# The second unit's decays from stacked rows, the first rows loaded between two halves of a weight block, two fills moved to GpSimd, other dummy matmuls

## The chip, the cores and the metric

The kernel runs on one core of one Trainium2 chip. The metric is the device time of one execution in microseconds (us). A profile of one execution comes with it: it says for each engine (TensorE, called PE, with its weight loads PEld; VectorE, DVE; ScalarE, ACT; GpSimd, POOL; and the DMA queue of SyncE, SP) what ran when and what it had waited for.

## What is computed

A chunked state-space scan over 4 batches, 8 heads and 768 positions, followed by a two-layer network. With `la = log(clip(a))`, and in every chunk:

```python
cum = np.cumsum(la, axis=-1)
L = np.exp(cum[:, :, :, None] - cum[:, :, None, :]) * causal
M = np.einsum('bhin,bhjn->bhij', Cc, Bc) * L
y = np.einsum('bhij,bhjd->bhid', M, xc) + (C state) * np.exp(cum)
state = exp(sum la) * state + sum_j (B_j x_j) * np.exp(cum[-1] - cum[j])
...
h = x @ w_in                      # 3072 x 256 times 256 x 2048
g = np.maximum(0.01 * h, h)
out = g @ w_out                   # 3072 x 2048 times 2048 x 256
```

The kernel takes chunks of 96 positions (`Q`), not of 32, which gives the same values.

## The kernel before

**Units.** The scan is cut into 32 units, each one chunk of 96 positions of one batch with its 8 heads. Unit `u` is batch `u % 4` of chunk `u // 4`. For each unit there are four steps:

1. *Decays.* PE writes the exponents of `L` (112 rows by 8 heads by 96 columns) into a PSUM tile `pd`; ACT takes the exponential into `lt` (`decay_of`, L276).
2. *Scores.* `scores` (L321) multiplies C and B for 4 heads at a time into a PSUM tile `sc`, of which there are two; DVE multiplies each half by `lt` (L326, two instructions).
3. *Products.* `unit_products` (L348 and L357, 8 small matmuls each) gives y and the new state in a `pd` tile, of which there are also two.
4. *Out.* ACT copies the state (`stage`, L381) and y (`xh`, L386), DVE takes the low part (`xl`, L391), and POOL carries the state into the next chunk's operand (L384).

**Three ways to the decays.** Units 0 and 1 (`DIRECT = 2`) go a direct way: a mask matmul in bf16 (`decay_mask`, L239), then an fp32 matmul with `reach`, a masked copy of `la` that POOL makes (`fill_reach`, L199; `decay_direct`, L246). Units 2 to 15 go by stacked rows (`decay_pe`, L265): one bf16 matmul for each half, whose operands `dl` and `dr` hold 0/1 masks and, in some of their rows, the cumulative sums of `la`, each split into three bf16 pieces. These rows are made so: PE sums (`sum_rows`, L221), DVE splits (`split_sums`, L227 to L230), one DMA stores the pieces to DRAM (`parts_d`, L618), and `decay_load` loads them back twice for a number of units, into `dl` (L254) and into `dr` (L257). There are 8 slots (`SLOTS`) for units; four units' rows at a time are loaded again later. Units from 16 on take their decays from a broadcast load. This change does not touch them.

**The order.** The order of instructions on each engine is written out by hand: no scheduler moves them. Each engine runs its own list in order and waits by semaphores; a DMA is issued in its place in the list of SP or ACT, and an issue that has to wait holds up what stands behind it on that queue. The prologue (L602 to L637) does the sums, the first units' decays and the first loads. The loop after it (L638) takes units 0 to 9: for unit `u` it does the decays of unit `u + 2`, the scores of unit `u + 1`, and the products of unit `u`, and in between parts of the decoding of the network's weights, which arrive as 64-bit floats in blocks of 512 KB (`fetch_w`, L100, into `raw`). After that the network's matmuls (`ffn_in`, L554, and `ffn_out`, L578) start, and the other units are woven between them.

**Dummies.** `keep_warm` (L128) issues matmuls of zeros, whose result is not used.

Of the kernel before, what the change touches and what calls it, by code (L numbers as in the profile page):

```python
# [13 lines left out]
U32 = mybir.dt.uint32  # L14
# [3 lines left out]
NB, NH, S, D, N = 4, 8, 768, 32, 16  # L18
Q = 96
# [9 lines left out]
B_COLS = NB * QE  # L29
LAG = 3  # L30
WARM = 6
WARM2 = 2
RAWS = 3
SHIFT = 448
LOAD = 4
# [9 lines left out]
POOLED = (0, 1, 2)  # L45
DRAWN = 3

DIRECT = 2
SLOTS = 8

STACKED_AT = {12: 0, 14: 2}
# [17 lines left out]
def scan_ffn(ctx: ExitStack, tc: tile.TileContext, a_l, b_l, c_l, bn_l, x_l, w_l, out_l):  # L69
# [25 lines left out]

    raws, bcs, xss, bns = {}, {}, {}, {}

    def fetch_w(f, eng=nc.sync):
        raws[f] = wr.tile([128, 2 * DM, 2], U32, name="raw")
        eng.dma_start(raws[f].rearrange("p c w -> p (c w)"), w_l[f].bitcast(U32))  # L100

    ccs = [pst.tile([128, 2, NB, Q], F32, name=f"cc{i}") for i in range(2)]

# [15 lines left out]
    def fetch_x(c, eng=nc.sync):  # L119
        eng.dma_start(xss[c][:Q].rearrange("p b c -> p (b c)"), x_l[c])  # L120
# [5 lines left out]
    def keep_warm(space, n):  # L126
        for _ in range(n):
            nc.tensor.matmul(  # L128
                space.rearrange("p (a b) -> p a b", b=128), lhsT=idle,
                rhs=idle.unsqueeze(1).to_broadcast([128, 4, 128]), start=True, stop=True,  # L130
            )
# [10 lines left out]
    for c in range(3):  # L142
# [35 lines left out]
        out=less, in_=less, pattern=[[3, NH]], compare_op=ALU.is_ge, fill=0.0, base=Q + 2,  # L178
        channel_multiplier=-1,
    )  # L180

    def fill_first():
        nc.vector.tensor_copy(dr[:Q, 0], later.unsqueeze(1).to_broadcast([Q, NH, Q]))

    def fill_less():
        rows = slice(Q, Q + 3 * NH)
        nc.scalar.copy(dr[rows, 0], less[rows].unsqueeze(2).to_broadcast([3 * NH, NH, Q]))

    def fill_slots(lo, hi):
        rows = slice(0, Q + 3 * NH)  # L190
        nc.vector.tensor_copy(
            dr[rows, lo:hi].rearrange("p b h i -> p b (h i)"),
            dr[rows, 0].rearrange("p h i -> p (h i)").unsqueeze(1).to_broadcast(
                [Q + 3 * NH, hi - lo, NH * Q]
            ),
        )

    def fill_reach(u):
        nc.gpsimd.affine_select(  # L199
            out=reach[u], in_=la[:, u * NH:(u + 1) * NH].unsqueeze(2).to_broadcast([Q, NH, Q]),  # L200
            pattern=[[0, NH], [1, Q]], compare_op=ALU.is_ge, fill=0.0, base=0,
            channel_multiplier=-1,
        )
# [33 lines left out]
    def decay_mask(space):  # L237
        for g in range(2):
            nc.tensor.matmul(  # L239
                heads_of(space, g), lhsT=upto_b,  # L240
                rhs=later.unsqueeze(1).to_broadcast([Q, NH // 2, Q]), start=True, stop=False,
            )

    def decay_direct(u, space):
        for g in range(2):
            nc.tensor.matmul(  # L246
                heads_of(space, g), lhsT=after, rhs=reach[u][:, 4 * g:4 * g + 4],
                start=False, stop=True,
            )

    def decay_load(u, n, eng=nc.sync):
        p, b = u * NH, (u - DIRECT) % SLOTS
        rows = parts_d[p:p + n * NH]
        nc.sync.dma_start(  # L254
            dl[Q:Q + 3 * NH, b:b + n, :Q], rows.rearrange("(u h) t i -> (h t) u i", h=NH)
        )
        eng.dma_start(  # L257
            dr[Q + 3 * NH:KD, b:b + n].rearrange("t b h i -> t (b h) i"),
            rows.rearrange("r t i -> t r i"),
        )  # L260

    def decay_pe(u, space):
        b = (u - DIRECT) % SLOTS
        for g in range(2):
            nc.tensor.matmul(  # L265
                heads_of(space, g), lhsT=dl[:KD, b], rhs=dr[:KD, b, 4 * g:4 * g + 4],
                start=True, stop=True,
            )
        decay_of(u, space)
        after_u = u + SLOTS - LOAD + 1  # L270
        if (u - DIRECT + 1) % LOAD == 0 and after_u < STACKED:
            decay_load(after_u, min(LOAD, STACKED - after_u))

    def decay_of(u, space):
        lt = lts[u] = plt.tile([QE, NH, Q], F32, name="lt")
        nc.scalar.activation(  # L276
            lt.rearrange("p (g h) i -> p g (h i)", g=2), space[:QE, :, :4 * Q], AF.Exp
        )
# [23 lines left out]
    def state_decay(c):  # L302
        nc.gpsimd.tensor_tensor(
            out=bns[c][:, :NB * NH * N].rearrange("p (h n) -> p h n", n=N),
            in0=bns[c][:, :NB * NH * N].rearrange("p (h n) -> p h n", n=N),
            in1=erev[:, c * NB * NH:(c + 1) * NB * NH].unsqueeze(2).to_broadcast([QE, NB * NH, N]),
            op=ALU.mult,
        )
# [3 lines left out]
    def scores(u, warm=0):  # L312
        c, b = divmod(u, NB)
        lt = lts[u].rearrange("p (g h) i -> p g (h i)", h=2)
        for half in range(2):
            sc = score_tile()
            if half == 0 and warm:
                keep_warm(sc[:, 0], warm)
            for g in range(2):
                r = 32 * (2 * half + g)  # L320
                nc.tensor.matmul(  # L321
                    sc[:QE, g, :2 * Q].rearrange("p (k i) -> p k i", k=2), lhsT=bcs[c][r:r + 32, b * QE:(b + 1) * QE],
                    rhs=ccs[c % 2][r:r + 32, :, b], start=True, stop=True,
                )
            heads = lt[:, 2 * half:2 * half + 2]
            nc.vector.tensor_tensor(out=heads, in0=sc[:QE, :, :2 * Q], in1=heads, op=ALU.mult)  # L326
# [270 lines left out]
    with tc.tile_pool(name="ps_d", bufs=2, space=PSUM, reuse_waits="tile") as ps_d:  # L597

        def free_tile():
            return ps_d.tile([128, 2, TS], F32, name="pd")  # L600

        nc.vector.tensor_scalar(  # L602
            out=la, in0=la, scalar1=1e-6, scalar2=1.0, op0=ALU.max, op1=ALU.min,
        )
        nc.scalar.activation(la, la, AF.Ln)
        pds = [free_tile() for _ in range(2)]
        second = score_tile()
        for u in range(DIRECT):
            fill_reach(u)
        nc.gpsimd.memset(ccs[1], 0.0)  # L610
        nc.vector.memset(dl[Q:], 1.0)
        nc.vector.memset(dl[Q:Q + 3 * NH, :, Q:], 0.0)
        fill_first()
        fill_less()
        prow = first[:, 0, :Q]
        sum_rows(prow, 0)
        split_sums(prow)
        nc.sync.dma_start(parts_d, parts)  # L618
        fetch_w(0)
        for u in range(DIRECT):  # L620
            decay_mask(pds[u])
        keep_warm(second[:, 1], WARM2)
        columns(erev, after, AF.Exp, second[:, 0])
        state_decay(0)
        decay_direct(0, pds[0])
        decay_of(0, pds[0])
        fill_slots(1, SLOTS // 2)
        scores(0)
        decay_direct(1, pds[1])
        nc.scalar.copy(dl[:Q], upto_b.unsqueeze(1).to_broadcast([Q, SLOTS, QE]))  # L630
        decay_load(DIRECT, 2, nc.scalar)
        decay_load(DIRECT + 2, SLOTS - 2)
        decay_of(1, pds[1])
        fill_slots(SLOTS // 2, SLOTS)
        fetch_bc(1)
        fetch_bn(1)
        fetch_x(1)  # L637
        for u in range(FIRST_UNITS):  # L638
            v = u + 2
            if u:  # L640
                decay_pe(v, free_tile())
            if u == 0:
                rest = unit_out(u, free_tile())
                rest()
            if u + 1 < FIRST_UNITS:
                scores(u + 1, int(0 < u < 4))
            else:
                pair_now((), (u + 1, u + 2))
                settle()
                state_decay(3)  # L650
                abs_more()
                pg = ctx.enter_context(tc.tile_pool(name="pg", bufs=LAG + 2))
                ffn_in(0, free_tile()[:, 0])
            if u:
                rest = unit_out(u, free_tile())
                rest()
            else:
                pd = free_tile()
                keep_warm(pd[:, 0], WARM2)
                decay_pe(v, pd)  # L660
            c, b = divmod(u, NB)
            if u == 1:
                fetch_w(1)
            if c + 2 <= 3:
                if b == 2:
                    fetch_bc(c + 2)
                if b == 3:
                    fetch_bn(c + 2)
            if u == 3:
                fetch_x(2)  # L670
            if u == 5:
                fetch_w(2)
            if u == 7:
                alloc_x(3)
                fetch_x(3)
            if u > 7:
                fetch_more()
            if u in (2, 5):
                state_decay(1 if u == 2 else 2)
            if u:  # L680
                settle()
            if u == 1:
                decode_abs(0)
            if u == 4:
                decode_abs(1)
            decode(LEAD.get(u, 0))
        ffn_act(0)
        ffn_low(0)
        decode(1)
# [323 lines left out]
```

## Time and profile before

| | before |
|---|---|
| time, three runs | 317.37 us median (316.97 to 318.34) |
| the profiled execution's own time | 318.41 us |
| its span in the profile | 316.7 us |
| busy in that span | PE 310.4 us, DVE 212.0, ACT 180.7, POOL 128.5 |
| weight loads (PEld) busy | 245.8 us |
| DMA | 26.29 MB, mean 83 GB/s |

The times in the profile count from the span's start. A row of the chain of waits has the start of a piece, its length and what ran in it. A row of the timeline has start, length, engine, source line and operation, and in brackets the idle time ahead of it with what ended it. Line numbers are those of the kernel before. PE is busy all through; its matmuls are pipelined and their ends are modelled, so its busy share does not tell how much of that work is needed.

### The profile page before, as it was taken

Reading aid. Unit: us, or ns where it says so; the run is one execution under the profiler, and the core shown is the slowest. Engines: PE = TensorE matmul, PEld = TensorE weight load, DVE = VectorE, ACT = ScalarE, POOL = GpSimd, SP = SyncE. Lnnn points to the kernel's source line nnn. Section 1 sums busy time; section 2 is a strip of 40 time slices with the busy share of each in tenths; the row PEclk is TensorE's granted clock in tenths of the full one; section 3 lists DMA queues with packets and bytes.
Section 4 is the critical chain, followed back from the end, with each engine's and each line's share of the span. In section 5 each row is a group of like instructions: output and inputs, shape, how many; then the busy total and the mean of one; then the engine's idle time right before and its main releaser. Section 6 shows DMA issues by size and latency. Waiting matters only on the chain.

```text
span 316.7 us, 6261 instructions
## 1 busy us (share of the span) xinstructions
PE 310.4 (98%) x2407; PEld 245.8 (78%) x2407; DVE 212.0 (67%) x350; ACT 180.7 (57%) x353; POOL 128.5 (41%) x215
## 2 busy tenths in 40 slices
PE   8999999999999999999999999999999999999995
PEld 4566877777888878888887878788887888888884
DVE  5697787898987677767634444277367676767561
ACT  3776776848574755646454634375365547645551
POOL 6288644614554242724434330070035466335100
PEclk9999999999999999999999999999999999999999
DMA  6987626094518322350204101000001000000003
GB/s 166 253 223 232 173 81 214 23 274 133 155 67 248 108 89 66 96 126 2 90 0 156 66 1 68 0 2 0 0 0 66 2 0 0 2 0 0 2 2 132
DMA packets 11722, 26.29 MB, mean 83 GB/s; under 512 B 2380, under 2 KB 4652, under 8 KB 11692
## 3 DMA queue, kind: packets, MB, share of 16 engines
q1 hardware_dynamic: 11641, 25.88, 27.3%
q8 instruction: 19, 0.31, 0.4%
q14 instruction: 11, 0.09, 0.1%
q10 hardware_dynamic: 51, 0.01, 0.0%
HBM read 22.57 MB, written 3.32 MB: 82 GB/s over the span
## 4 chain that ended last, share of the span: by engine, by line
PE 95%; DVE 2%; ACT 1%; issue 1%; DVEq 0%; ACTq 0%
PE op L578 27%; PE hp L554 26%; PE sc L800 9%; PE op L820 7%; PE sc L820 6%; PE hp L800 3%; PE sc L411 3%; PE sc L348 3%; PE sc L321 2%; PE pd L348 1%; PE pd L265 1%; PE sc L128 1%; PE pd L246 1%; DVE w L465 1%; PE sc L357 1%
## 5 line engine op out<-in xcount | busy, mean ns | idle before, releaser
L567 DVE TENSOR_TENSOR gl<-hp,gh 128x512 fp32r<-128x512 f32 x63 | 43.4, 689 | 55.4 <-ACT hp L564 55.3
L561 ACT ACTIVATE gh<-hp 128x512 fp32r<-128x512 f32 x63 | 37.6, 598 | 63.0 <-PE hp L554 62.9
L578 PE MATMUL op<-gh,wh 128*128 128x512 f32 x128 | 50.9, 398 | 0.0
L554 PE MATMUL hp<-xh,wh 128*128 128x512 f32 x126 | 50.0, 397 | 0.4 <-DVE gl L567 0.4
L578 PE MATMUL op<-gh,wl 128*128 128x512 f32 x128 | 49.9, 390 | 0.0
L578 PE MATMUL op<-gl,wh 128*128 128x512 f32 x128 | 49.8, 389 | 0.0
L554 PE MATMUL hp<-xl,wh 128*128 128x512 f32 x126 | 49.2, 390 | 0.0
L554 PE MATMUL hp<-xh,wl 128*128 128x512 f32 x126 | 49.2, 390 | 0.0
L384 POOL COPY xs<-stage 16x64 f32<-16x64 f32 x112 | 30.8, 275 | 30.5 <-ACT stage L381 25.9
L766 POOL TENSOR_TENSOR sl<-s,sh 128x512 fp32r<-128x512 f32 x8 | 10.4, 1295 | 71.3 <-ACT sh L765 71.3
L564 ACT ACTIVATE hp<-hp 128x512 f32<-128x512 f32 x63 | 37.5, 595 | 0.0
L297 POOL TENSOR_SCALAR_AFFINE_SELECT lt<-lt 96x768 f32<-96x768 f32 x16 | 15.7, 982 | 47.8 <-ACT lt L296 47.8
L288 POOL TENSOR_TENSOR lt<-lt,ccol 112x768 f32<-112x768 f32 x16 | 25.2, 1577 | 10.8 <-DMA lt<-crow_d 6.0
L578 PEld LDWEIGHTS op<-gh,wh 128*128 128x128 f32 x128 | 24.0, 188 | 7.0 <-issue 1.4
L554 PEld LDWEIGHTS hp<-xh,wh 128*128 128x128 f32 x126 | 23.7, 188 | 5.9 <-DVE gl L567 0.8
L578 PEld LDWEIGHTS op<-gl,wh 128*128 128x128 f32 x128 | 24.0, 188 | 5.1
L554 PEld LDWEIGHTS hp<-xl,wh 128*128 128x128 f32 x126 | 23.6, 188 | 5.4 <-DVE xl L391 0.5
L578 PEld LDWEIGHTS op<-gh,wl 128*128 128x128 f32 x128 | 24.0, 188 | 4.6
L554 PEld LDWEIGHTS hp<-xh,wl 128*128 128x128 f32 x126 | 23.7, 188 | 4.8 <-DVE wl L485 0.2
L424 DVE TENSOR_TENSOR lt<-sc,lt 112x384 f32<-112x384 f32 x44 | 21.6, 548 | 3.5 <-ACT xh L386 1.8
L833 DVE TENSOR_TENSOR gl<-c,gh 128x512 fp32r<-128x512 f32 x24 | 23.1, 962 | 1.0 <-ACT c L830 0.7
L829 ACT ACTIVATE gh<-hp 128x512 fp32r<-128x512 f32 x8 | 4.8, 600 | 27.2 <-PE hp L800 27.2
(164 smaller groups left out, 617.0 us busy)
## 6 DMA issues: line engine op xcount, KB each, us to landing
raw<-w_l SPq DMA_DIRECT2D x16, 512.0 KB, 3.3
lt<-crow_d SPq DMA_DIRECT2D x16, 336.0 KB, 4.6
xs<-x_l SPq DMA_DIRECT2D x8, 384.0 KB, 8.2
out_l<-ob SPq DMA_DIRECT2D x12, 256.0 KB, 2.2
bn<-bn_l SPq DMA_DIRECT2D x8, 231.0 KB, 3.8
bt<-b_l SPq DMA_DIRECT2D x8, 224.0 KB, 6.4
cc<-c_l SPq DMA_DIRECT2D x16, 96.0 KB, 4.6
la<-a_l SPq DMA_DIRECT2D x1, 96.0 KB
```

What stands on the lines that cost most here:

```text
L288: nc.gpsimd.tensor_tensor(out=lts[u], in0=lts[u], in1=ccol[:, u * NH:(u + 1) * NH].unsqueeze(2).to_broadcast([QE, NH, Q]), op=ALU.subtract,)
L297: nc.gpsimd.affine_select(out=lt[:Q], in_=lt[:Q], pattern=[[0, NH], [1, Q]], compare_op=ALU.is_ge, fill=0.0, base=0, channel_multiplier=-1,)
L384: nc.gpsimd.tensor_copy(to[:, :, hh], stage[hh * D:hh * D + N])
L424: nc.vector.tensor_tensor(out=heads, in0=spaces[half][:QE, :, 2 * Q * e:2 * Q * (e + 1)], in1=heads, op=ALU.mult,)
L554: nc.tensor.matmul(hp, lhsT=w_half[half][:, f, k * 128:(k + 1) * 128], rhs=x[t][:, k, :], start=(n == 0), stop=(n == 5),)
L561: nc.scalar.activation(ghs[s], hp, AF.Prelu, alpha=0.01)
L564: nc.scalar.activation(hps[s], hps[s], AF.Prelu, alpha=0.01)
L567: nc.vector.tensor_tensor(out=gls[s], in0=hps.pop(s), in1=ghs[s], op=ALU.subtract)
L578: nc.tensor.matmul(op, lhsT=w_half[half][:, f, DM + m * 128:DM + (m + 1) * 128], rhs=x, start=(first and i == 0), stop=(last and i == 2),)
L800: nc.tensor.matmul(bank, lhsT=w[h], rhs=x[g], start=start and i == 0, stop=i == 2, skip_group_check=True,)
L820: nc.tensor.matmul(outs[t][m], lhsT=w_half[half][:, f, DM + m * 128:DM + (m + 1) * 128], rhs=x, start=first and i == 0, stop=last and i == 2,)
L833: nc.vector.tensor_tensor(out=gl, in0=g, in1=gh, op=ALU.subtract)
```

## The change

The first weight block is fetched in two halves of 256 KB, with the first load of stacked rows between them. `DIRECT` falls from 2 to 1, so unit 1 takes its decays by stacked rows, and its mask and direct matmuls and its `reach` go. The first row load covers three units (1 to 3) and its `dr` half on ACT's queue is issued ahead of the exponential of unit 0. Two fills of `dl` move from DVE to POOL, and the copy into `dl` on ACT moves ahead to the prologue's start. The slots are counted from unit 1, so that the later loads are issued one unit earlier. Of dummies, `WARM2` is 3 in place of 2 in the prologue; the two ahead of unit 2's decays now stand ahead of unit 1's; and the one in front of unit 4's scores goes.

```diff
-WARM2 = 2
+WARM2 = 3
-DIRECT = 2
+DIRECT = 1
...
-    def fetch_w(f, eng=nc.sync):
-        raws[f] = wr.tile([128, 2 * DM, 2], U32, name="raw")
-        eng.dma_start(raws[f].rearrange("p c w -> p (c w)"), w_l[f].bitcast(U32))
+    def fetch_w(f, half=None):
+        if f not in raws:
+            raws[f] = wr.tile([128, 2 * DM, 2], U32, name="raw")
+        part = slice(0, 2 * DM) if half is None else slice(half * DM, (half + 1) * DM)
+        nc.sync.dma_start(
+            raws[f][:, part].rearrange("p c w -> p (c w)"),
...
+    nc.gpsimd.memset(dl[Q:], 1.0)
+    nc.gpsimd.memset(dl[Q:Q + 3 * NH, :, Q:], 0.0)
...
-        for u in range(DIRECT):
-            fill_reach(u)
+        fill_reach(0)
         nc.gpsimd.memset(ccs[1], 0.0)
-        nc.vector.memset(dl[Q:], 1.0)
-        nc.vector.memset(dl[Q:Q + 3 * NH, :, Q:], 0.0)
         fill_first()
         fill_less()
+        nc.scalar.copy(dl[:Q], upto_b.unsqueeze(1).to_broadcast([Q, SLOTS, QE]))
         prow = first[:, 0, :Q]
         sum_rows(prow, 0)
         split_sums(prow)
         nc.sync.dma_start(parts_d, parts)
-        fetch_w(0)
-        for u in range(DIRECT):
-            decay_mask(pds[u])
+        fetch_w(0, 0)
+        decay_mask(pds[0])
         keep_warm(second[:, 1], WARM2)
         columns(erev, after, AF.Exp, second[:, 0])
         state_decay(0)
+        decay_load(DIRECT, 3, nc.scalar)
         decay_direct(0, pds[0])
         decay_of(0, pds[0])
         fill_slots(1, SLOTS // 2)
         scores(0)
-        decay_direct(1, pds[1])
-        nc.scalar.copy(dl[:Q], upto_b.unsqueeze(1).to_broadcast([Q, SLOTS, QE]))
-        decay_load(DIRECT, 2, nc.scalar)
-        decay_load(DIRECT + 2, SLOTS - 2)
-        decay_of(1, pds[1])
-        fill_slots(SLOTS // 2, SLOTS)
+        fetch_w(0, 1)
+        decay_load(DIRECT + 3, SLOTS - 3)
         fetch_bc(1)
         fetch_bn(1)
         fetch_x(1)
+        keep_warm(pds[1][:, 0], 2)
+        decay_pe(1, pds[1])
+        fill_slots(SLOTS // 2, SLOTS)
...
-                scores(u + 1, int(0 < u < 4))
+                scores(u + 1, int(0 < u < 3))
...
-                pd = free_tile()
-                keep_warm(pd[:, 0], WARM2)
-                decay_pe(v, pd)
+                decay_pe(v, free_tile())
```

What this does to the order on three engines is seen in their lists. On PE the place is the stretch from unit 0's direct decays to the end of unit 1's scores. In the kernel before it reads (L246 are direct decays, the first pair unit 0's and the second unit 1's; L321 scores; L348 and L357 products of unit 0; L128 the dummies, L265 the decays of unit 2):

```order
L246 MATMUL pd<-lt,after 112x384 x2
L321 MATMUL sc<-cc_95,bt 112x192 x4
L246 MATMUL pd<-lt,after 112x384 x2
L348 MATMUL pd<-lt,xs 32x96 x8
L357 MATMUL pd<-xs,bn 32x32 x8
L321 MATMUL sc<-cc_95,bt 112x192 x4
L128 LDWEIGHTS idle
L128 MATMUL pd<-idle 128x512
```

And in the changed kernel, whose lines have other numbers (L255 direct decays of unit 0, L330 scores, L135 dummies, L274 decays by stacked rows, L357 and L366 products):

```order
L255 MATMUL pd<-lt,after 112x384 x2
L330 MATMUL sc<-cc_95,bt 112x192 x4
L135 LDWEIGHTS idle
L135 MATMUL pd<-idle 128x512
L135 LDWEIGHTS idle
L135 MATMUL pd<-idle 128x512
L274 LDWEIGHTS dl
L274 MATMUL pd<-dr,dl 112x384
L274 LDWEIGHTS dl
L274 MATMUL pd<-dr,dl 112x384
L357 MATMUL pd<-lt,xs 32x96 x8
L366 MATMUL pd<-xs,bn 32x32 x8
```

The products of unit 0 now stand behind decays that read `dl` and `dr`, and with that behind the first load of rows; the dummies have come ahead of both.

On ACT the place is the prologue. Before, from the copy of `less` on (L218 is an exponential of all units' sums, L276 the exponentials of units 0 and 1, L630 the copy into `dl`, L257 the load of the rows of units 2 and 3 into `dr`):

```order
L187 COPY dr<-less 24x768
L218 ACTIVATE erev<-sc 112x256
L276 ACTIVATE lt<-pd 112x768
L630 COPY dl<-upto_b 96x896
L257 DMA dr<-parts_d 3x16x96
L276 ACTIVATE lt<-pd 112x768
```

And in the changed kernel (L266 is now the load of units 1 to 3, L285 the two exponentials):

```order
L196 COPY dr<-less 24x768
L621 COPY dl<-upto_b 96x896
L227 ACTIVATE erev<-sc 112x256
L266 DMA dr<-parts_d 3x24x96
L285 ACTIVATE lt<-pd 112x768 x2
```

The copy has moved two places forward and the load one exponential forward, and the load is half as large again.

On SP the place is what stands behind the store of the pieces (L618 before, L625 after). Before, with L100 the weight block, L254 and L257 the row loads into `dl` and `dr`, and L106 the next chunk's B:

```order
L618 DMA parts_d<-parts 128x288
L100 DMA raw<-w_l 128x1024
L254 DMA dl<-parts_d 24x2x96
L254 DMA dl<-parts_d 24x6x96
L257 DMA dr<-parts_d 3x48x96
L106 DMA bt<-b_l 128x448
```

And in the changed kernel (L102 the weight halves, L263 and L266 the row loads, L113 the next chunk's B):

```order
L625 DMA parts_d<-parts 128x288
L102 DMA raw<-w_l 128x512
L263 DMA dl<-parts_d 24x3x96
L102 DMA raw<-w_l 128x512
L263 DMA dl<-parts_d 24x5x96
L266 DMA dr<-parts_d 3x40x96
L113 DMA bt<-b_l 128x448
```

One issue has come in, the second half of the weight block, ahead of the rows of units 4 to 8.

More of the change, by code (lines that the diff above doesn't have):

```diff
@@ L96, in scan_ffn @@
     raws, bcs, xss, bns = {}, {}, {}, {}
-    def fetch_w(f, eng=nc.sync):
-        raws[f] = wr.tile([128, 2 * DM, 2], U32, name="raw")
-        eng.dma_start(raws[f].rearrange("p c w -> p (c w)"), w_l[f].bitcast(U32))
+    def fetch_w(f, half=None):
[4 more added lines that the diff above has]
+            raws[f][:, part].rearrange("p c w -> p (c w)"),
+            w_l[f].bitcast(U32).rearrange("p (c w) -> p c w", w=2)[:, part].rearrange(
+                "p c w -> p (c w)"
+            ),
+        )
     ccs = [pst.tile([128, 2, NB, Q], F32, name=f"cc{i}") for i in range(2)]
```

## Prediction

> **What bounds the kernel now.** I read the page's chain by engine first, then the chain of waits in order of time over the stretch that the change touches, then the timeline there.
>
> ```profile
> PE 95%; DVE 2%; ACT 1%; issue 1%; DVEq 0%; ACTq 0%
> ```
>
> The end is set by PE nearly all the way, so anything that makes PE start its later work sooner or later by some amount moves the end by that amount, unless a wait in between absorbs it. All that the change touches lies before 17 us. The chain there:
>
> ```profile
> 3.80 0.61 PE sc L221 x2
> 4.41 1.28 PE pd L239 x4
> 5.69 0.72 PE sc L128 x2
> 6.41 0.43 PE sc L217 x2
> 6.84 1.29 PE pd L246 x4
> 8.13 0.52 PE sc L321 x8
> 8.65 1.47 PE pd L246 x4
> 10.13 0.47 PE pd L348 x16
> 10.60 0.12 PE pd L357 x16
> 10.72 0.52 PE sc L321 x8
> 11.24 0.54 PE pd L128 x2
> 11.78 0.69 PE pd L265 x4
> 12.47 0.22 PE sc L128
> 12.69 0.57 PE sc L321 x8
> 13.25 0.47 PE pd L348 x16
> 13.85 0.46 PE pd L265 x2
> ```
>
> PE stands there without a gap. But beside it other engines are nearly as late:
>
> ```profile
> 8.16 0.81 ACT L276 ACTIVATE lt<-pd 112x768 f32<-112x768 f32 x1 [0.91 <-PE pd L246]
> 9.01 1.02 DVE L326 TENSOR_TENSOR lt<-sc,lt 112x384 f32<-112x384 f32 x2 [1.93 <-ACT lt L276]
> 10.16 0.81 ACT L276 ACTIVATE lt<-pd 112x768 f32<-112x768 f32 x1 [0.23 <-PE pd L246]
> 11.61 1.01 DVE L326 TENSOR_TENSOR lt<-sc,lt 112x384 f32<-112x384 f32 x2
> 15.15 1.02 DVE L326 TENSOR_TENSOR lt<-sc,lt 112x384 f32<-112x384 f32 x2 [0.41 <-PE sc L321]
> 16.18 0.36 DVE L391 TENSOR_TENSOR xl<-pd,xh 128x192 fp32r<-128x192 f32 x1
> 17.25 1.02 DVE L326 TENSOR_TENSOR lt<-sc,lt 112x384 f32<-112x384 f32 x2
> ```
>
> Unit 0's products cannot start before DVE has multiplied its scores, at 9.01 + 1.02 = 10.03; PE reaches them at 10.13. So of the 1.47 us of unit 1's direct matmuls (8.65 to 10.13) only 0.1 us is more than cover for ACT and DVE. From 15.15 on DVE works without a break, in which a shorter PE list brings nothing.
>
> **The change part by part.** Let T be the time at which PE can start unit 1's decays by stacked rows, that is when the first row load has landed. All hangs on it.
>
> *PE up to there.* One mask goes (1.28 / 2 = 0.64), one dummy comes (0.72 / 2 = 0.36), so the direct decays of unit 0 start some 0.2 earlier (0.28 by these rows, 0.1 if the dummies in that place run as slowly as the first six). They end near 7.9, unit 0's scores near 8.45, the two dummies that moved (0.54) near 9.0. Then PE waits until T.
>
> *When the load starts.*
>
> ```profile
> 3.34 0.81 DVE L611 MEMSET dl<- 32x896 bf16 x1 [0.24 <-issue]
> 4.37 0.36 DVE L183 COPY dr<-later 96x768 bf16<-96x768 bf16 x1
> 4.64 0.25 DVE L227 CAST parts<-sc 128x96 bf16<-128x96 f32 x1
> 5.84 0.35 SPq L618 DMA_DIRECT2D parts_d<-parts  x1
> 7.78 0.75 SPq L254 DMA_DIRECT2D dl<-parts_d  x2
> ```
>
> Without the fills DVE copies `later` a microsecond earlier, and the split can begin when PE's sums end, at 4.41, not at 4.64. The gain is between 0 (if a hand-over eats it) and 0.23; I take 0.16. The store goes out at 5.68, and the load, 7.78 − 5.84 = 1.94 behind it, at 7.62.
>
> *How long the load takes.* No view gives the landing of these rows, so it is bounded from both sides. The nearest rows:
>
> ```profile
> 8.23 0.51 ACTq L257 DMA_DIRECT2D dr<-parts_d  x1
> 11.66 0.81 PE L265 MATMUL pd<-dr,dl 123*112 123x384 bf16 x4
> ```
>
> From ACT's issue of two units' rows to the first matmul that reads them are 11.66 − 8.23 = 3.43 us, dummies ahead of it included, so that load took at most 3.43. At the other end stands the store of the pieces, a transfer of the same data whose release came 1.94 after its issue. What ran on the DMA engines in between:
>
> ```profile
> 9.00:9.50 0.50, 0.50 (x3) 0.35 (x2) 0.49 (x2) 0.50 (x1) 0.00 (x0) 1.00 0.27 59
> 9.50:10.00 0.50, 0.50 (x2) 0.00 (x0) 0.50 (x3) 0.44 (x1) 0.00 (x0) 1.00 0.39 71
> ```
>
> In this microsecond only 59 and 71 GB/s moved: small rows, once the weight block was through. The new load is of the same kind as that of the upper end and half as large again, but has half the weight block ahead of it; I put it nearer the upper end, at 2.8. So **T = 7.62 + 2.8 = 10.4**, between 9.6 (1.94) and 11.05 (3.43).
>
> *From T on.* Unit 1's decays take PE 0.46 (the row at 13.85), the products 0.47 + 0.12, unit 1's scores 0.52, two units' decays 0.69, a dummy 0.22, unit 2's scores 0.57: T + 3.05 for unit 1's products, which stood at 13.25. The two dummies that are out of this row (0.54) are the gain. But there are two score tiles, so the second half of unit 2's scores waits until DVE has multiplied both halves of unit 1's. In the rows of before that product begins 11.61 − 10.16 = 1.45 after unit 1's exponential and takes 1.01; the exponential now starts at T + 0.46 and a hand-over of 0.03, so DVE is done at T + 2.95, and half of 0.57 and a hand-over behind it unit 1's products start at **T + 3.3**. This is what decides: 13.25 is met at T = 9.95, and each later microsecond costs one. At T = 10.4 it is 13.7: **0.45 later**.
>
> *What is queued behind the wait.* On PE, unit 0's products, unit 1's scores and all units after them; ACT's state copy and DVE's low part of unit 0 wait for those. ACT itself stands until the store has landed (7.62) and issues the load (0.51) ahead of unit 0's exponential: 8.13, where it began at 8.16, so nothing (at the two ends: 0.5 earlier if the issue runs beside it, 0.16 later if the store gains nothing), and T covers it.
>
> *Edits that I cost at nothing, with their cover.*
>
> ```profile
> 0.80 0.74 POOL L133 MEMSET cc<- 128x768 f32 x1 [0.29 <-POOLq L1002]
> 3.62 1.84 POOL L199 TENSOR_SCALAR_AFFINE_SELECT lt<-la 96x768 f32<-96x768 f32 x2 [0.92 <-ACT la L605]
> 14.24 0.68 ACT L445 ACTIVATE w<-raw 128x512 f32<-128x512 f32 x1
> ```
>
> The fills on POOL, by the row at 0.80 between nothing and some 0.9 each, lie in its idle 0.92 and then push unit 0's `reach` from 4.54 to 5.5 at most, wanted at 6.6; without that cover they would cost what goes beyond. The copy into `dl` fills ACT's idle time after 4.4. The second weight half, one issue later on SP, is wanted first at 14.24; the next chunk's loads, 0.4 later at most, by unit 4's scores, after 15.15. The later row loads come one unit earlier for units one earlier. The dummy of unit 4's scores (0.22) lies where DVE has no break: nothing, at most 0.22 gained.
>
> **Sum.** +0.45 on the profiled 318.41 (span 316.7 and 1.7 around it) is 318.9. That execution was 1.04 above the median of the runs, 317.37; on that median the forecast is **317.8**.
>
> The Trainium skill has a rule against this load (DMA: Bandwidth & Descriptors, "Why a DMA increments its semaphore by 16 and not by 1"): a DMA runs on as many engines as divide its slowest dimension on both sides, up to 16. That of the `dr` rows is 3, so by that page they run on three engines, and the time should grow with the rows; this is what the second rival would come from, and no view of before shows it.
>
> **The rivals.**
>
> *The load is quick* (T at 9.6). For it: less is ahead of it than before. Then unit 1's products start at 12.9, 0.35 earlier, and the time is 317.0. PE's shorter list cannot bring more, since unit 0's product on DVE still ends near 10.0.
>
> *The load goes by its number of rows; it ends on the slower side.* Of 3.43, some 0.9 is the way until small rows move (8.23 to the window at 9.00 and a little); if the remaining 2.5 is by rows, three units' take 3.8 and T is 7.62 + 0.9 + 3.8 = 12.3. PE stands from 9.0 to 12.3, unit 1's products start at 15.6, and the time is 317.37 + 2.35 = 319.7. It counts as slower from T = 11.55. Against it: the 3.43 is an upper bound, with dummies until just before its end, and another load of six units' rows ran at the same time; here the next load is issued a microsecond later.
>
> *The removed PE work shows in full* (the load is hidden, and DVE and ACT move up too). Gone are 0.64 + 1.47 + 0.22, come are 0.36 + 0.46: 1.5 less, 315.9. Against it stands the product at 10.03.
>
> *The clock falls in the wait.* PE will be without work for up to 2 us, and dummies are fewer. What this trace shows of the rate:
>
> ```profile
> 1.06 2.74 PE sc L128 x6
> 31.50 0.36 issue
> ```
>
> A dummy takes 2.74 / 6 = 0.46 at the start, 0.36 at 5.69 and 0.22 at 12.47: half rate at first, full rate after some 4.6 us of work. If the wait threw PE back, it would run at half rate for as long again and lose 2.3: 320.1 with the forecast's delay. The longest piece without work on the chain is 0.36 long, so no row tells whether 1.4 us is enough for that. The Trainium skill (TensorE: Matmul & The Clock Gate, "Part 1: The HAM clock gate (the "warmup" mystery)") says that the clock falls after an idle window of about 3.4 us; by that page this wait is too short and costs nothing more.
>
> **How the numbers follow.** The forecast (T from 9.95 to 11.5) 0.58, the quick load 0.27, the load by rows 0.09, the work in full 0.03, the clock 0.03. A measurement of this kernel can tell 0.5%, 1.6 us. Slower by more are the load by rows and the clock: 0.12. Faster by more is half of the work in full, which lies at that border: 0.015, given as 0.02. Same: the rest, 0.86. The range takes in the bounds of T, −0.35 to +1.1 on 317.37, and 0.4 and 0.5 for the scatter of a median of three (316.97 to 318.34): 316.6 to 319.0. Left out are the load by rows, the work in full and the clock, 0.15.
>
> **What would show it.** The first decay matmuls of unit 1 at 10.4 with an idle stretch of over a microsecond ahead of them on PE; unit 0's exponential near 8.1; unit 1's products near 13.7; the store's issue near 5.7; and from 17 on the same rows as before, all shifted by the same amount. If the decays start before 9.9, the quick load is right; if unit 1's products do not follow T by 3.3, the wait for DVE is wrong; if the shift at 13.7 is gone at 40, something later absorbs it, and the forecast falls with its mechanism in place.

## The result, and the profile after

| kernel | executions | median us | lowest to highest |
|---|---|---|---|
| before | 6 | 317.71 | 316.97 to 318.80 |
| changed | 6 | 319.44 | 319.06 to 319.87 |
| changed, measured again beside another set of runs | 12 | 319.62 | 319.14 to 323.30 |

The changed kernel takes 1.0054 times as long (95% interval 1.0031 to 1.0077), and 1.0072 (1.0042 to 1.0102) in the repeat. By the medians that is 1.7 to 1.8 us, where 0.45 were forecast; the time lies 0.4 above the range. With three more executions the kernel before came to 317.71, 0.34 above the 317.37 on which the range was built, so most of the excess over the range, though not of the loss, is that base. The profiled executions agree with the loss: span 318.1 now, 316.7 before. All medians and ratios here and below leave out five executions in a slow state (324 to 1462 us), the profiled one of e5 among them.

The first lines to read are those of the running sum of the first chunk's rates, which stands ahead of everything. In the timeline of before (start, length, engine, line, operation, tiles, and in brackets the idle time ahead and what ended it):

```profile
2.81 0.29 DVE L602 TENSOR_SCALAR la<-la 96x256 f32<-96x256 f32 x1 [0.68 <-DMA la<-a_l]
3.13 0.42 ACT L605 ACTIVATE la<-la 96x256 f32<-96x256 f32 x1 [1.05 <-DVE la L602]
3.69 0.71 PE L221 MATMUL sc<-upto,la 96*128 96x96 f32 x2
```

And in the timeline of the changed kernel, with the later rows that the prediction named:

```profile
2.75 0.84 POOL L188 MEMSET dl<- 32x896 bf16 x1
2.84 0.90 DVE L611 TENSOR_SCALAR la<-la 96x256 f32<-96x256 f32 x1 [0.71 <-DMA la<-a_l]
3.77 0.42 ACT L614 ACTIVATE la<-la 96x256 f32<-96x256 f32 x1 [1.69 <-DVE la L611]
4.33 0.71 PE L230 MATMUL sc<-upto,la 96*128 96x96 f32 x2 [0.53 <-ACT la L614]
6.21 0.35 SPq L625 DMA_DIRECT2D parts_d<-parts  x1
10.23 0.60 PE L135 MATMUL pd<-idle 128*128 128x512 bf16 x2
10.67 0.49 PE L274 MATMUL pd<-dr,dl 123*112 123x384 bf16 x2
```

The clamp of the rates (`la`) on DVE is the same instruction on the same data, and it takes 0.90 instead of 0.29. Beside it, on POOL, runs the fill of `dl` that the change put there; the fill ends at 3.59, the clamp at 3.74. The logarithm and PE's sums come 0.64 later, and PE, which has its six dummies behind it at 3.80, stands idle for 0.53.

The chain of waits of the changed kernel (start, length, what) shows what follows:

```profile
5.69 1.28 PE sc L135 x3
6.97 0.85 PE sc L226 x2
7.82 1.97 PE pd L255 x4
...
9.81 0.82 ACT lt L285
...
10.65 1.03 DVE lt L335 x2
...
11.73 0.37 PE pd L357 x8
...
12.75 0.92 PE pd L274 x4
...
14.69 0.47 PE pd L357 x16
```

Against the prediction's rows of before: three dummies take 1.28, 0.43 each, where two took 0.72; the columns take 0.85 instead of 0.43; the four direct decay matmuls 1.97 instead of 1.29. These are the same instructions at half rate. (The column of the granted clock reads 1.00 there, so the rate is read from like instructions.) At full rate the 1.97 would be 1.29, so half rate lasts 2 × (1.97 − 1.29) = 1.36 into them, to 9.2; before, it ends inside the second of the two dummies, near 6.2. PE reaches full rate 3 us later. Unit 0's exponential starts at 9.81 instead of 8.16, and unit 1's products at 14.69 instead of 13.25. At the end the two profiles are again 1.4 apart (318.1 − 316.7), but the 1.44 does not travel there unchanged: like rows of the two chains are 1.01 apart at 36 us (36.22 and 37.23) and 1.63 at 51 (51.21 and 52.84). Between 24 and 44 us the engines' turns shift against each other, by some tenths of a microsecond, which the forecast did not expect.

The wait for the first rows, on which the forecast rests, is not in this chain: PE's decays by stacked rows start at 10.67 right behind the dummies, so T is at most 10.67 (forecast 10.4), and the chain goes past them through ACT and DVE of unit 0.

### The profile page after: what moved, and what is told of

It reads as the page before. It is cut to its first block, busy times and chain, and to the rows that moved or that the text cites. A ratio compares the mean times of both kernels' runs of the same rounds, so it can differ in the third digit from the quotient of the medians.

```text
span 318.1 us, 6253 instructions
## 1 busy us (share of the span) xinstructions
PE 311.3 (98%) x2403; PEld 246.2 (77%) x2403; DVE 211.7 (67%) x348; ACT 180.7 (57%) x353; POOL 129.1 (41%) x216
## 4 chain that ended last, share of the span: by engine, by line
PE 90%; DVE 5%; ACT 2%; issue 1%; DMA 1%; DVEq 0%; ACTq 0%
PE op L587 26%; PE hp L563 24%; PE sc L804 9%; PE op L824 7%; PE sc L824 6%; PE hp L804 3%; PE sc L420 3%; PE sc L357 3%; PE sc L330 2%; PE pd L274 1%; DVE w L474 1%; PE pd L357 1%; ACT lt L285 1%; PE sc L366 1%; DMA la<-a_l 1%
## 5 line engine op out<-in xcount | busy, mean ns | idle before, releaser
L770 POOL TENSOR_TENSOR sl<-s,sh 128x512 fp32r<-128x512 f32 x8 | 10.4, 1298 | 71.3 <-ACT sh L769 71.3
L297 POOL TENSOR_TENSOR lt<-lt,ccol 112x768 f32<-112x768 f32 x16 | 26.0, 1625 | 9.9 <-DMA lt<-crow_d 7.1
```

Source lines behind the costliest of these rows:

```text
L297: nc.gpsimd.tensor_tensor(out=lts[u], in0=lts[u], in1=ccol[:, u * NH:(u + 1) * NH].unsqueeze(2).to_broadcast([QE, NH, Q]), op=ALU.subtract,)
```

## The experiments

Two theories were to be told apart. In the first, **the fill**, POOL's fill holds the clamp, the hole in PE keeps its rate down, and all the loss follows from that. In the second, **the row wait**, PE loses by its wait for the first rows, through the wait's length or through what it does to PE's clock. (The first expectations call them A and B.)

| run | what it is | median us (beside before) | ratio, 95% |
|---|---|---|---|
| e1 | changed, fills on DVE, old place | 319.52 (317.43) | 1.0063 (1.0038 to 1.0089) |
| e2 | before, fills on POOL | 320.06 (317.43) | 1.0079 (1.0053 to 1.0105) |
| e3 | changed, one dummy more at the start | 320.40 (317.43) | 1.0095 (1.0065 to 1.0125) |
| e4 | before, one dummy fewer at the start | 319.43 (317.43) | 1.0067 (1.0046 to 1.0087) |
| e5 | changed, fills on DVE behind the split | 318.40 (317.67) | 1.0028 (1.0012 to 1.0044) |
| e6 | e5 and eight dummies in the row wait | 318.07 (317.67) | 1.0014 (0.9996 to 1.0032) |
| e7 | e5, first load of one unit's rows | 318.48 (317.67) | 1.0027 (1.0010 to 1.0044) |
| e8 | changed, fills on POOL behind `reach` | 318.92 (317.67) | 1.0042 (1.0024 to 1.0060) |
| e9 | e5, unit 1 direct as before | 318.73 (317.79) | 1.0029 (1.0007 to 1.0050) |
| e10 | changed, dummies in hole and row wait | 319.33 (317.79) | 1.0043 (1.0011 to 1.0075) |
| e11 | changed, again | 319.62 (317.79) | 1.0072 (1.0042 to 1.0102) |

### The fill alone, and the hole alone

e2 is the kernel before with only the fills moved:

```
+    nc.gpsimd.memset(dl[Q:], 1.0)                        # behind the fills of `less`
+    nc.gpsimd.memset(dl[Q:Q + 3 * NH, :, Q:], 0.0)
...
-        nc.vector.memset(dl[Q:], 1.0)
-        nc.vector.memset(dl[Q:Q + 3 * NH, :, Q:], 0.0)
```

> The kernel before with only the two fills of dl moved to POOL, nothing else of the change. Theory A: the clamp takes 0.9 us, PE's hole ahead of the sums is 0.5 us; if the clock then rises late, unit 0's direct decays run at half rate and the time is 1.2 to 1.8 us above the kernel before; if the clock does not depend on the hole, only 0.6 us above. Theory B: no change of time, within 0.3 us.

e4 is the kernel before with the hole alone: the fills stay on DVE, and one dummy at the start goes.

```
-WARM = 6
+WARM = 5
```

> The kernel before with one dummy fewer at its start (5 in place of 6), so that PE has a hole of about 0.4 us ahead of the sums while the clamp and all sums keep their time. If a hole of that size holds the clock's rise up: unit 0's direct decays run at half rate and the time is 0.7 to 1.2 us above the kernel before. If not: the same time within 0.3 us.

The chain of waits of e2:

```profile
2.88 0.88 DVE la L604
...
7.18 0.85 PE sc L219 x2
8.03 1.68 PE pd L248 x4
...
9.81 3.86 DMA dr<-parts_d
...
13.71 0.81 PE pd L267 x4
```

And of e4:

```profile
2.80 0.30 DVE la L602
...
6.53 0.85 PE sc L217 x2
7.38 1.77 PE pd L246 x4
...
9.24 4.21 DMA dr<-parts_d
...
13.48 0.81 PE pd L265 x4
```

And from the timeline of e4, the hole:

```profile
3.68 0.71 PE L221 MATMUL sc<-upto,la 96*128 96x96 f32 x2 [0.31 <-ACT la L605]
```

Moving the fills alone gives the clamp its 0.88 and costs 2.6 us. (In e2 the third step of the split is held as well, for 1.05 at 5.67 beside POOL's next fill, so the store goes out at 7.04; the chain passes this by.) But in e4 the clamp takes its 0.30, and still the columns take 0.85, the direct decays 1.77, and 2.0 us are lost: one dummy of 0.46 less at the start, which leaves PE idle for 0.31, is enough. So the held clamp costs mainly through the hole that it opens in PE, and the hole through the late full rate. Both losses are larger than expected (at most 1.8 and 1.2). In the kernel before, the load of unit 2's rows stands behind unit 0's exponential on ACT, so it starts late too (9.81 and 9.24 instead of 8.23), and unit 2's decays come at 13.71 and 13.48, not 11.78. In the changed kernel this load stands ahead of the exponential, which may be why the hole costs less there; the intervals overlap, and no run tests it.

### The fills off the clamp, three places

e1 puts the two fills back on DVE, at the place where they stood before:

```
-    nc.gpsimd.memset(dl[Q:], 1.0)
-    nc.gpsimd.memset(dl[Q:Q + 3 * NH, :, Q:], 0.0)
...
         nc.gpsimd.memset(ccs[1], 0.0)
+        nc.vector.memset(dl[Q:], 1.0)
+        nc.vector.memset(dl[Q:Q + 3 * NH, :, Q:], 0.0)
```

> The changed kernel with its two fills of dl back on DVE, ahead of the copy of later, all else as changed. Theory A (the fill on POOL holds DVE's clamp of la back, all sums come 0.6 us later, PE has a hole of 0.5 us ahead of them and its clock rises some 3 us later): the clamp is back to about 0.3 us, the exponent's log starts at 3.1, the two fp32 passes of unit 0's direct decays end near 8.0 at full rate, and the time is within 0.5 us of the kernel before. Theory B (the wait for the row load, as predicted): nothing of that matters, T stays near 10.7 and the time stays 1.4 to 1.7 us above the kernel before.

e5 puts them on DVE right behind `split_sums(prow)`; e8 leaves them on POOL, behind `fill_reach(0)`.

> The changed kernel with its two fills of dl on DVE behind the split of the sums, so that neither the clamp nor the split is held up. Theory A (two causes side by side, of which the later decides: POOL's fill with the late clock, and the row load) says: clamp 0.3 us, full rate from about 6.3, the pieces' store near 5.7, the load's landing T near 10.0 (7.55 and the 2.4 that the load took with the fills back in their old place), unit 1's products at T + 3.3 to T + 3.6 = 13.3 to 13.6, time 0 to 0.5 us above the kernel before in executions with the full clock, and more in those in which PE's wait of 1.3 us lets the clock fall. If the load alone explained the loss: the same time as the changed kernel.

> The changed kernel with its two fills still on POOL, but behind the making of reach, so that they start near 4.5 and not while DVE clamps. Theory A: the clamp takes 0.3 us, PE has no hole ahead of the sums, the direct decays run at full rate; the split may be held up by up to 0.2 us where a copy from SBUF meets the fill; time as with the fills behind the split, within 0.5 us. If the fills on POOL cost by being there at all: the time of the changed kernel.

The timeline of e1:

```profile
2.80 0.29 DVE L609 TENSOR_SCALAR la<-la 96x256 f32<-96x256 f32 x1 [0.67 <-DMA la<-a_l]
3.61 0.87 POOL L206 TENSOR_SCALAR_AFFINE_SELECT lt<-la 96x768 f32<-96x768 f32 x1 [0.92 <-ACT la L612]
4.35 1.02 DVE L190 COPY dr<-later 96x768 bf16<-96x768 bf16 x1
4.43 0.73 POOL L616 MEMSET cc<- 128x768 f32 x1
6.39 0.35 SPq L625 DMA_DIRECT2D parts_d<-parts  x1
10.50 0.48 PE L272 MATMUL pd<-dr,dl 123*112 123x384 bf16 x2 [1.38 <-DMA dr<-parts_d]
```

The clamp is back at 0.29 and PE at full rate, and now the forecast's wait is there: 1.38 of idle PE, T at 10.50, and unit 1's products at 14.11, T + 3.61. But the median, 319.52, did not fall, against what the fill theory alone expected. Two things are in it. The copy of `later` now runs beside another fill of POOL and takes 1.02 where it took 0.36, so the split and the store come late (6.39). And the executions differ: the five with a mean granted clock of 0.998 or more took 318.22 to 319.71 (median 318.35), the other seven with 0.993 to 0.995 took 318.72 to 322.14 (median 320.12). So a part of the row-wait theory is right: in some executions the clock falls, and, as e8 and e6 will show, it falls behind that wait.

e8 shows this in its profile. The wait, in the timeline, and then the stretches of 11 to 16 us (window, its length, busy time and count of PE, PEld, DVE, ACT, POOL, granted clock, DMA share, GB/s):

```profile
2.84 0.29 DVE L609 TENSOR_SCALAR la<-la 96x256 f32<-96x256 f32 x1 [0.70 <-DMA la<-a_l]
9.92 0.48 PE L272 MATMUL pd<-dr,dl 123*112 123x384 bf16 x2 [1.59 <-DMA dr<-parts_d]
```

```profile
11.00:12.00 1.00, 1.00 (x10) 0.66 (x11) 0.61 (x3) 0.58 (x3) 0.44 (x2) 0.71 0.80 269
12.00:13.00 1.00, 1.00 (x5) 0.39 (x3) 0.90 (x2) 0.62 (x1) 0.49 (x3) 0.50 0.78 150
13.00:14.00 1.00, 1.00 (x9) 0.46 (x8) 0.00 (x0) 0.89 (x2) 0.00 (x0) 0.50 1.10 349
14.00:15.00 1.00, 1.00 (x38) 0.74 (x32) 0.56 (x2) 0.00 (x0) 0.00 (x0) 0.59 1.11 238
15.00:16.00 1.00, 1.00 (x27) 0.55 (x19) 0.74 (x2) 0.74 (x3) 0.43 (x2) 1.00 0.89 270
```

PE waited 1.59, worked again from 9.92, and 1.5 us later its clock went to 0.5 for some 3.4 us. One such fall takes the mean clock of a span of 317 us to 1 − 3.4 × 0.5 / 317 = 0.995. Six of the eleven executions had a mean clock of 0.995 (median 319.34; the other five 318.65). In e5 the fills run beside none of these instructions, and the wait stays: three of its eleven were at 0.994 or 0.995 and took 319.0 to 320.0, the other eight had a median of 318.35. That is 0.68 above the kernel before at the full clock, where 0 to 0.5 was expected; e5 has no profile that could say more.

### The hole filled, the row wait left

e3 is the changed kernel with one dummy more at the start:

```
-WARM = 6
+WARM = 7
```

> The changed kernel with one more dummy at its very start (7 in place of 6, each 0.43 to 0.46 us), which fills PE's hole ahead of the sums. The clamp stays at 0.9 us. If the hole is what makes the clock rise late: the dummies ahead of the sums of decays run at half rate only until about 6.3 us, unit 0's direct decays take 1.3 us, and the time is 0.8 to 1.1 us below the changed kernel. If the clock rises when it does for another reason (a grid in time that the span does not show): no change, within 0.3 us. Theory B: no change.

The chain of waits of e3, and its timeline where PE goes on:

```profile
1.06 3.17 PE sc L135 x7
...
4.33 0.71 PE sc L230 x2
...
6.28 0.45 PE sc L226 x2
```

```profile
12.15 0.71 PE L274 MATMUL pd<-dr,dl 123*112 123x384 bf16 x2 [3.08 <-DMA bt<-b_l]
```

The clamp is held as in the changed kernel and the sums start at 4.33, but PE idles only 0.10 ahead of them, the three dummies behind the mask take 0.65, and the columns 0.45: full rate is there by 5.63, no later than in the kernel before. That part held. The time did not: 320.40 is 1.0 above the changed kernel, not 0.8 to 1.1 below. PE came to the rows early, waited 3.08 for them, and its granted clock was 0.50 to 0.65 in the four microseconds from 12 to 16. (The wait ends with the load into `dr` by all that PE reads there, for its weights from `dl` were loaded at 10.17; the B named in the bracket is not read by these matmuls.) Five of six executions had 0.995 or less. Filling one hole opened the other.

### The row wait covered

e6 is e5 with

```
-        keep_warm(pds[1][:, 0], 2)
+        keep_warm(pds[1][:, 0], 8)
```

> The same with 8 dummies in place of 2 ahead of unit 1's decays (six more of 0.22 us), so that PE works while it waits for the rows, until about 10.2. If the spread that the run with the fills in their old place showed (318.2 to 322.1) comes from the clock falling after the wait: all executions within 1 us of each other, mean clock 0.998 or more, median at or below that of the run without these dummies. If it comes from the load's own time: the same spread.

The chain of waits of e6:

```profile
6.57 1.29 PE pd L253 x4
...
8.38 1.83 PE pd L135 x8
10.22 0.33 PE pd L272 x2
...
13.67 0.47 PE pd L355 x16
```

All twelve executions had a clock of 0.998 or more, against three low ones of eleven in e5, seven of twelve in e1 and six of eleven in e8 (and one of twelve in e7 below, with four dummies): the dummies in the wait keep the clock up. But the twelve still spread from 317.40 to 319.83, where all within 1 us were expected, so the clock is not the only source of scatter.

Unit 1's products come at 13.67 (forecast 13.7, before 13.25), and the median is 0.40 us up (forecast 0.45). How near these are is in part luck. The start of the decays at 10.22 is set by the eight dummies and not by the rows, which had landed by then; the interval of the ratio reaches from 0.1 us below the kernel before to 1.0 above; and in the profiles the delay does not last. At 51 us e6 is 0.34 ahead of the kernel before (50.87 and 51.21), and its span is 0.5 shorter (316.2 and 316.7). So the delay at unit 1 is shown, and its way to the end is not.

e10 keeps the fills on POOL and puts in both covers: `WARM = 7` and the eight dummies.

> The changed kernel as it is, fills on POOL, but with 7 dummies at the start (which fill PE's hole ahead of the sums) and 8 in place of 2 ahead of unit 1's decays (which fill PE's wait for the rows). POOL's fill still holds the clamp up by 0.6 us, so the pieces are stored at 6.2 and not at 5.7, but the clock rises near 6.3 and does not fall. If the clock (late rise or fall, whichever of the two comes) is what the change lost beyond the forecast: mean clock 0.998 or more, T near 10.5, time 0.4 to 0.9 us above the kernel before. If the fill on POOL costs in another way too: as the changed kernel, 1.4 us or more above.

Its profiled execution starts unit 1's products at 14.22, which is e6's 13.67 and the 0.55 by which its dummies end later (10.77, not 10.22). That is 0.97 behind the kernel before. Its clocks were 0.998 or more. But its median is 1.5 above the kernel before, not 0.4 to 0.9, and its times run from 317.66 to 321.88, so the interval, 0.4 to 2.4 us, decides little; why it scatters so was not found.

### Two other parts of the change

e7 shortens the first load, from three units' rows to one, on e5 with four dummies:

```
-        decay_load(DIRECT, 3, nc.scalar)
+        decay_load(DIRECT, 1, nc.scalar)
+        decay_load(DIRECT + 1, 2)
...
-        keep_warm(pds[1][:, 0], 2)
+        keep_warm(pds[1][:, 0], 4)
```

> The same as the first of this call, but the first load brings the rows of unit 1 alone (8 rows for each of the three pieces in place of 24), those of units 2 and 3 come by a second load on SP's queue, and 4 dummies stand ahead of unit 1's decays. If the load's time goes by its rows: T near 9.2, 0.8 or more earlier than with three units, and the time 0.2 to 0.6 us below the kernel before, since the products of unit 0 then start near 10.0. If it is a fixed delay: T near 10, time as in the first of this call.

The chain of waits of e7:

```profile
5.43 3.17 DMA parts_d<-parts
...
8.69 1.71 DMA dl<-parts_d
...
10.54 0.50 PE pd L272 x2
```

The load took 1.71 (its `dl` half, on which PE waited here), against 1.95 in e8 and 2.38 in e1 for three units (the `dr` half), but the store before it took 3.17 here, 2.04 in e8 and 1.60 in e1. What the store varies by is more than what rows could save: the dependence on rows is not settled, and nothing was gained.

e9 undoes the named part of the change on e5: unit 1's decays direct again (`DIRECT = 2`, both masks, `WARM2 = 2`, no dummies ahead of unit 2's decays), with the early load and the half blocks kept.

> The changed kernel with unit 1 back on the direct way (mask, fp32 matmuls, two dummies in the prologue as before), the fills of dl on DVE behind the split, the first load (units 2 and 3) still ahead of unit 0's exponential and between the weight halves, and no dummies ahead of unit 2's decays. No wait for a load should then stand on PE: the load lands near 10.2, unit 2's decays come at 11.2. If the loss was the wait for unit 1's rows and nothing else of the change: unit 0's products stay at 10.1, unit 1's products come 0.3 earlier than in the kernel before (13.0), and the time is 0 to 0.5 us below it. If the halves of the weight block or the moved loads cost by themselves: 0.3 us or more above.

The timeline of e9:

```profile
3.64 1.70 POOL L206 TENSOR_SCALAR_AFFINE_SELECT lt<-la 96x768 f32<-96x768 f32 x2 [0.95 <-ACT la L612]
4.91 1.18 DVE L236 CAST parts<-rest 128x96 bf16<-128x96 f32 x1
5.29 0.73 POOL L617 MEMSET cc<- 128x768 f32 x1
6.41 0.35 SPq L626 DMA_DIRECT2D parts_d<-parts  x1
8.10 0.50 ACTq L264 DMA_DIRECT2D dr<-parts_d  x1
8.65 1.51 ACT L283 ACTIVATE lt<-pd 112x768 f32<-112x768 f32 x2 [2.42 <-DMA parts_d<-parts]
```

No row wait, clock 0.998 or more in eleven of twelve, and still 0.9 us over before. The split's third step took 1.18, not 0.21, beside POOL's fill of `cc`, so the store went out at 6.41; and since the load now stands ahead of unit 0's exponential on ACT, that one waited 2.42 for the store to land and 0.50 for the issue. It began 0.49 later than before, and unit 1's products at 13.53, not 13.25. That is 0.28 of the 0.9; like rows are 0.67 apart at 30 us (29.31 and 29.98), and what adds the rest is not known. So e9 does not clear the halves of the weight block and the moved loads. No version beat the kernel before.

## Why the prediction was wrong

- **The step that failed: "The fills on POOL ... lie in its idle 0.92".** It asked whether POOL had time, and not who else was held while POOL worked. The moved fill held DVE's clamp, an early link of the chain, for 0.6 us; through the hole in PE it delayed full rate by 3 us, and unit 1's products by 1.44, for which the forecast had put nothing. By the medians, the fills at their place on POOL are worth 1.0 of the loss (the changed kernel at +1.73, and +1.83 in e11; e5 at +0.73), by the ratios 0.8; the intervals overlap, so the size is loose. The Trainium skill has the rule (SBUF — State Buffer, "Who interferes with whom"): DVE's `copy`, `cast` and `tensor_scalar` can take a port pair that DVE shares with GpSimd, and the loser stands for the whole instruction. This case agrees: 0.29 against 0.88 to 0.95 with the fill beside it. The prediction did not weigh it.
- **The rival that was priced too low: "The clock falls in the wait", 0.03.** Its cost was put too high (2.3 forecast; by the medians, executions with a low clock lie above the others by 1.8 in e1, 1.2 in e5 and 0.7 in e8), its chance too low. The clocks (low in seven of twelve in e1, six of eleven in e8, three of eleven in e5, in none of e6's twelve) and the windows of e8 and e3 show the thing itself. What it is worth on a median goes by how often it comes: in e1 the median is +2.1 and +0.9 without the low clocks, in e5 +0.73 and +0.68. The prediction leaned on the Trainium skill's 3.4 us of idle (TensorE: Matmul & The Clock Gate, "Part 1: The HAM clock gate (the "warmup" mystery)"); here the fall came behind a wait of 1.59. In the two profiles of the changed kernel PE comes late, has no wait for the rows and keeps its clock. But six of the twelve executions of e11 had a low mean clock, though none of the first six; since none of these was profiled, where their clock fell is not known.
- **PE up to there, and the store.** Forecast: unit 0's direct decays end near 7.9, store at 5.68, unit 0's exponential at 8.13. Measured: 9.79, 6.21, 9.81. All three are the late clamp and the late rate. In e6, without the collision, the decays end at 7.86 and the store goes out at 5.54.
- **T and what hangs on it held, up to unit 1's products.** T was 10.50 in e1, 9.92 in e8 and at most 10.67 in the changed kernel, against 10.4; e3's 12.15 alone lies outside 9.6 to 11.05. Unit 1's products followed by 3.61 in e1 (the rest is a dummy that took 0.36, not 0.22, and small gaps) against 3.3. So this term was right in its mechanism and near in size. Its last step, that the shift at 13.7 is the shift at the end, is not borne out: in e6's profile the shift is gone at 51 us, which the prediction itself had named as a way to fail with its mechanism in place.
- **Quick load, load by rows, work in full.** No run gave T of 9.6; e8 came nearest with 9.92, and e3's one profile has 12.15, 4.3 behind the load's issue, for which no row gives a cause; "work in full" is refuted by the chain through unit 0's exponential and product, which sets unit 0's products in the changed kernel (11.73) and in e9 (10.57).
- **The sum.** 0.40 (e6, without collision and with the wait covered) + 0.33 (e5 less e6, the uncovered wait) + 1.00 (changed less e5, the fills) = 1.73. This is a ledger of medians, and differences taken in a row add up whatever the causes are. In the changed kernel the terms do not stand side by side: in its profile the chain is the hole's, and the wait for rows is hidden under it.

What stays open: a pause of 0.60 of PE at 39.48 in e1's chain, which no wait in the profile explains; why the store takes 1.6 to 3.2 us and the load of rows 1.7 to 4.2; and the scatter of e10. In e11 four executions at a mean clock of 0.994 or 0.995 took 319.55 to 320.52, hardly more than the 319.14 to 320.22 of the six at 0.998 and over; the two at 0.989, by the reckoning above two falls, took 322.78 and 323.30, the longest of all.

## What to carry to other kernels

Before a fill goes to an engine because that engine is idle, look at what the neighbour engine runs in the same microsecond: here a fill of 0.84 beside an early link of the chain cost its own length or more at the end (0.8 to 1.0 us in the changed kernel, 2.6 in e2). In the first microseconds of this kernel PE's rate hung on unbroken work, so dummies must reach to the latest time at which their successor can start, and a wait that a change adds on PE needs dummies as well as a price. When a cost is given as nothing "because it is hidden", test the cover from both sides: who is idle, and who is held.

## What the runs showed of the hardware

- **POOL's fills hold some DVE instructions.** Beside a fill the clamp took 0.88 to 0.95 (0.29 alone), the copy 1.02 (0.36), the cast from SBUF 1.18 in e9 and 0.43 in e8 (0.21 in e1); each ended 0.07 to 0.21 behind the fill. Taken back by its own length, each begins 0.14 or 0.15 ahead of the fill's recorded end: the clamp at 3.74 − 0.29 = 3.45 (fill to 3.59), e1's copy at 5.37 − 0.36 = 5.01 (5.16), e9's cast at 6.09 − 0.21 = 5.88 (6.02). So each was held whole and then ran at its own speed, and POOL's records seem to end that much late. In e1 and e9 the DVE instruction is recorded as started ahead of the fill (4.35 against 4.43, 4.91 against 5.29). But a select of POOL was still running then (3.61 to 4.48, 3.64 to 5.34), and e9's cast, at 0.21, would have been over ahead of that fill: a select seems to hold as well. The Trainium skill (SBUF — State Buffer, "Who interferes with whom") says that whoever is first keeps the pair; these rows agree. In the kernel before the copy took its 0.36 beside two selects of POOL, but the second of these took 1.01, not 0.88; it looks as if the copy came between them and the select waited.
- **A hole of 0.3 to 0.5 us in PE's work between 3.4 and 4.3 us delays full rate by 2 to 3 us.** By the direct decays (1.97, 1.60 and 1.77 against 1.29) half rate lasted to 9.2 in the changed kernel, 8.4 in e11, 8.3 in e4, against 6.2. All eight profiles without such a hole (the kernel before, e1, e3, e6 to e10) run these decays at full rate, all four with it (the changed kernel, e2, e4, e11) begin them at half rate.
- **The clock can fall after short waits, and late.** It fell after 1.59 (e8) and 3.08 (e3) of waiting, and not in the profiles of e1 and e7 after 1.38 and 1.03; in e8 not in the wait but 1.5 us into the work behind it, for 3.4 us.
